# Batch 0's phi and K over two queues in head halves, and the constants of ones on GpSimd, at the start of a fused attention and channel-mix kernel

## The chip, the cores and the metric

The kernel runs on one core of a Trainium2 chip. Five engines work beside each other, each on its own list of instructions: TensorE (PE in the profile, its weight loads PEld), VectorE (DVE), ScalarE (ACT), GpSimd (POOL) and SyncE (SP), which only issues DMAs here. The metric is device time in microseconds, the median of several runs; lower is better.

## What is computed

For each of 8 batches and 8 heads, 576 tokens of width 64 attend through 32 memory slots; the result goes through a gated channel mix (d_model 512, d_ff 1024).

```python
# attention: q, k, v (8, 8, 576, 64), phi (8, 8, 576, 32)
a = exp(phi - max);  a = a / (sum(a, axis=2) + 1e-09)
k_m = einsum('bhsm,bhsd->bhmd', a, k);  v_m = einsum('bhsm,bhsd->bhmd', a, v)
attn = softmax(scale * q @ k_m.T)
x = (attn @ v_m)            # heads side by side: (8, 576, 512)
# channel mix
xk = mu_k * x + (1 - mu_k) * x_prev;   xr = mu_r * x + (1 - mu_r) * x_prev
k = relu(xk @ w_k);   v = k * k @ w_v;   r = sigmoid(xr @ w_r)
out = r * v
```

## The kernel before

The order of all work is written out by hand. `PLAN` (L19 to L85) is one long list of words; the loop at L800 runs through it and issues what each word stands for. `0:mu` is a step of batch 0, `c0:6a` a block of the key matmul, `b:1x8@3` a number of filler matmuls (`keep_busy`, L255, into PSUM bank 3), `p:q:0b` a preload. A word that comes twice is a step in two parts: the matmuls, and later what unloads them. Each engine works through its instructions in the order of issue; a wait for data stops everything behind it on that engine. PE's list at the start, by PLAN, is: 10 fillers of 512 columns (`WARM`, L262), three more, the transpose of mu (`0:mu`, L276), two fillers, the sums of exp(phi) (`0:z`, L321), six fillers, the K products of head groups 0 and 1 (`0:kg0`, L311), three fillers, those of head groups 2 and 3 (`0:kg1`), one filler, the broadcast of mu (`0:mub`, L267), and so on. The fillers multiply a tile of zeros and their results are not used.

Batch 0 is loaded first, ahead of PLAN. Phi goes as one DMA of 576 KB on ScalarE's queue (`load_phi`, L182), then K as two DMAs of 576 KB each, head groups 0 and 1, then 2 and 3 (`k0`, L184 and L185). Both arrive as float32. SyncE's queue carries mu_k and mu_r, 2 KB each, into `mu2` (L188, L189). ScalarE then takes exp of phi, second half of the head groups first (`0:exp1`, `0:exp0`, L291). K is turned to bf16 by `cast_k` (L296): groups 0, 1 and 2 on ScalarE (`0:c00`, `0:c01`, `0:c10`), group 3 on VectorE (`0:c11`), where the cast stands ahead of the copy of mu (L278) and the reciprocal of the sums (L325). `kg0` needs c00 and c01, `kg1` needs c10 and c11.

GpSimd issues all other loads, which change float32 to bf16 on the way. Its list begins with `PRE` (L91, run at L230):

```python
PRE = "after: id: q:0a"
```

`after` copies one element of `mu2` into `mark` (L211), a tile that nothing reads, so that GpSimd goes on when mu is in; `id` makes the identity matrix (a memset and a select); `q:0a` is the first part of q of batch 0. PLAN's preloads follow (q's second part, V in two halves, the weights, phi of batch 1 and so on).

VectorE clears `zeros` (L186), which the fillers read, then casts from the identity (`ident_f`, `sel`) and writes two constants: `ones` (L236 and L238, three memsets), the right-hand side of `0:z`, and `sumh` (L243 and L246, five memsets), which the denominators (L419) use.

Of the kernel before, what the change touches and what calls it, by code (L numbers as in the profile page):

```python
# [10 lines left out]
F32 = mybir.dt.float32  # L11
BF16 = mybir.dt.bfloat16
# [75 lines left out]

WARM = (10, 8)

PRE = "after: id: q:0a"  # L91
TAIL = ("o:72",)
WHOLE = {"o:71a": "scalar", "o:71b": "sync"}
ONE = ("o:32", "o:30", "o:33", "o:31", "o:42",)
# [3 lines left out]
NJ = 9  # L98
# [5 lines left out]
def kernel(  # L104
# [13 lines left out]
    nc = tc.nc  # L118
    B, H, S, D = q.shape
    M = phi.shape[-1]  # L120
# [15 lines left out]
    const = ctx.enter_context(tc.sbuf_pool(name="const", bufs=1))  # L136
    big = ctx.enter_context(tc.sbuf_pool(name="big", bufs=1))
    ld = ctx.enter_context(tc.sbuf_pool(name="ld", bufs=2))
# [19 lines left out]
    HH = H // 2  # L158
    ROWS = (slice(0, 64), slice(64, 128))
# [2 lines left out]
    q0s = [const.tile([128, HH, w, D], BF16, name=f"q0{w}") for w in (5, 4)]  # L162
    ems = [const.tile([128, NJ, HH, M], BF16, name=f"em{i}") for i in range(2)]
    identity = const.tile([128, 128], BF16, name="identity")
    mark = const.tile([1, 1], F32, name="mark")
    zeros = const.tile([128, 128], BF16, name="zeros")


    loads = {}

    def rows(src):
        return src.rearrange("h s d -> (h s) d").rearrange("(a p j) d -> p a (j d)", a=HH, j=NJ)

    def load_phi(b, eng):
        ph = ld.tile([128, HH, NJ, M], F32, name="ph", tag="ph")
        eng.dma_start(out=ph.rearrange("p h j m -> p h (j m)"), in_=rows(phi[b]))
        loads[b] = ph

    def load_rows(dst, src):
        nc.gpsimd.dma_start(out=dst.rearrange("p h j d -> p h (j d)"), in_=rows(src))  # L180

    load_phi(0, nc.scalar)  # L182
    k0 = work.tile([128, HH, NJ, D], F32, name="k0f", tag="G", bufs=2)
    for gs in (slice(0, 2), slice(2, 4)):  # L184
        nc.scalar.dma_start(out=k0[:, gs].rearrange("p h j d -> p h (j d)"), in_=rows(k[0])[:, gs])  # L185
    nc.vector.memset(zeros, 0.0)  # L186
    mu2 = const.tile([2 * ND, 128], F32, name="mu2")
    nc.sync.dma_start(out=mu2[:ND, :], in_=moe_mu_k.rearrange("(a b) -> a b", b=128))  # L188
# [12 lines left out]
    def preload(word):  # L201

        what, _, part = word.partition(":")
        if what in weights:
            dst, src = weights[what]
            f0, f1 = (int(x) * 128 for x in part.split("-"))
            nc.gpsimd.dma_start(out=dst[:, :, f0:f1], in_=src[:, :, f0:f1])
        elif what == "id":
            make_identity(nc, identity)
        elif what == "after":  # L210
            nc.gpsimd.tensor_copy(mark, mu2[:1, :1])  # L211
        else:
            n = int(part[0])
            if what == "phi":
                load_phi(n, nc.gpsimd)
            else:
                dst = qs[n % 2].rearrange("p (h j) d -> p h j d", j=NJ) if what == "q" else kvs[n % 2][:, "kv".index(what)]
                src = {"q": q, "k": k, "v": v}[what][n]
                if part[1:] in ("a", "b"):
                    x = "ab".index(part[1])  # L220
                    js = HALVES[x]
                    nc.gpsimd.dma_start(out=q0s[x].rearrange("p h j d -> p h (j d)"),
                                        in_=rows(src)[:, :, js.start // QR * D:js.stop // QR * D])
                elif part[1:] in ("g", "h"):
                    gs = slice(0, 2) if part[1] == "g" else slice(2, 4)
                    nc.gpsimd.dma_start(out=dst[:, gs].rearrange("p h j d -> p h (j d)"), in_=rows(src)[:, gs])
                else:
                    load_rows(dst, src)

    for word in PRE.split():  # L230
        preload(word)

    ident_f = const.tile([2 * ND, 2 * ND], F32, name="identf")
    nc.vector.tensor_copy(ident_f, identity[:2 * ND, :2 * ND])
    ones = const.tile([128, 2], BF16, name="ones")
    nc.vector.memset(ones, 0.0)  # L236
    for hg in range(2):
        nc.vector.memset(ones[ROWS[hg], hg:hg + 1], 1.0)  # L238

    sel = const.tile([2 * ND, 2 * HH, M], F32, name="sel")  # L240
    nc.vector.tensor_copy(sel, identity[:2 * ND, :2 * HH].unsqueeze(2).to_broadcast([2 * ND, 2 * HH, M]))
    sumh = const.tile([128, 4, M], BF16, name="sumh")
    nc.vector.memset(sumh, 0.0)  # L243
    for g in range(4):
        r = slice(g * M, (g + 1) * M)
        nc.vector.memset(sumh[r, g, :], 1.0)  # L246
    mu1 = const.tile([128, 2 * ND], F32, name="mu1")
    mu_m = const.tile([128, 2, 2, 2, D], F32, name="mu_m")

# [550 lines left out]
    for word in " ".join(PLAN).split():  # L800
        word, _, used = word.partition("@")
        word, _, now["by"] = word.partition("/")
        now["banks"] = iter(used)
        who, _, name = word.partition(":")
        if who == "p":
            preload(name)
        elif who == "w":
            queues[:] = [nc.sync]
            store(name, outs[name], slice(0, Dm))
        elif who == "b":  # L810
            keep_busy(*map(int, name.split("x")))
        else:
            now["whole"] = word in WHOLE or word in ONE
            if word in WHOLE:
                queues[:] = [getattr(nc, WHOLE[word])]
            elif len(queues) != 1 + (word in TAIL) or queues[0] is not nc.sync:
                queues[:] = [nc.sync, nc.scalar][:1 + (word in TAIL)]
            parts = pending.pop(word, None) or (mixes[who][name] if who in mixes else attend[int(who)](name))()
            if hasattr(parts, "send") and next(parts, who) is not who:
                pending[word] = parts  # L820
# [31 lines left out]
```

## Time and profile before

| what | value |
|---|---|
| time, median of 3 runs | 189.22 us (189.16 to 189.24) |
| span of the profiled execution | 187.4 us |
| median less span | 1.8 us |
| packets of the software queue (GpSimd's loads) | 20.45 MB, 59.1% of 16 engines' span |
| packets of ScalarE's queue (q10) | 2.08 MB, 3.4% |
| packets of SyncE's queue (q1) | 9.00 MB, 17.3% |

The span runs from the first to the last instruction of one execution taken by the hardware profiler. The time of that execution by itself is not among the numbers; the median is that of unprofiled runs of the same kernel. A row of the timeline or of the chain gives the start and the duration in us, then engine, line and operation; x9 means nine instructions merged into one row, whose duration reaches from the first start to the last end. In square brackets stands how long the engine was idle before, and what ended the wait. ACTq, SPq and POOL with DMA_DIRECT2D are issues of DMAs, not the transfers. A filler's row is "idle L258": that is the name of its PSUM tile; PE works then.

### The profile page before, as it was taken

The page shows a single profiled execution, that of the slowest core. Times are in us where ns is not written, and L with a number is a line of the kernel's source. Part 1 is how long each engine was busy: PE and PEld are TensorE (multiplying, and loading weights), DVE is VectorE, ACT ScalarE, POOL GpSimd, SP SyncE. Part 2 cuts the span into 40 slices and gives each one's busy share as a digit, 9 for nine tenths or more (in the row PEclk, how much of TensorE's full clock was granted, in tenths as well). Part 3 has the DMA queues.
Part 4 walks back from the last instruction along what each step waited for, and adds up shares of the span by engine and source line. Part 5 has one row for each costly group of instructions (what it writes and reads, how often), then busy time and mean ns, then how long its engine had stood idle before and what let it go on. Part 6 is the DMA issues. An engine that isn't in the chain of part 4 may idle for free.

```text
span 187.4 us, 5998 instructions
## 1 busy us (share of the span) xinstructions
PE 180.2 (96%) x2459; PEld 102.9 (55%) x2481; DVE 158.9 (85%) x344; ACT 146.5 (78%) x352; POOL 30.0 (16%) x46
## 2 busy tenths in 40 slices
PE   7998998999999999999999999999999999999992
PEld 2454764667645565556554755655535563474451
DVE  2265877999999999999999999987999999989441
ACT  2638866879999999999998999868998887656500
POOL 5843522121310450110103000000000000000000
PEclk9999999999999999999999999999999999999998
DMA  5999999999999999999999992142203421240254
GB/s 181 288 204 270 203 207 203 252 222 208 287 218 272 231 230 344 258 268 270 272 180 155 200 263 66 33 112 59 58 0 80 93 59 43 70 112 3 56 139 141
DMA packets 24940, 31.91 MB, mean 170 GB/s; under 512 B 1897, under 2 KB 19057, under 8 KB 24913
## 3 DMA queue, kind: packets, MB, share of 16 engines
q0 software_dynamic: 17936, 20.45, 59.1%
q1 hardware_dynamic: 5680, 9.00, 17.3%
q10 hardware_dynamic: 1296, 2.08, 3.4%
q8 instruction: 19, 0.31, 0.6%
q14 instruction: 9, 0.07, 0.1%
HBM read 38.28 MB, written 9.44 MB: 255 GB/s over the span
## 4 chain that ended last, share of the span: by engine, by line
PE 96%; issue 1%; ACT 1%; DVE 1%; ACTq 0%
PE pv L759 33%; PE pk L616 8%; PE pk L624 7%; PE pb L624 7%; PE idle L258 7%; PE gps L491 6%; PE kvps L311 4%; PE pk L598 4%; PE pb L686 3%; PE pr L686 3%; PE pr L678 3%; PE pr L708 2%; PE scps L394 2%; PE pr L665 2%; PE zps L321 1%
## 5 line engine op out<-in xcount | busy, mean ns | idle before, releaser
L759 PE MATMUL pv<-wv,sq 128*128 128x512 bf16 (+3 forms) x285 | 59.3, 350 | 0.5
L759 PEld LDWEIGHTS <-sq 128*128 128x128 bf16 x296 | 27.6, 98 | 25.6 <-issue 2.4
L497 ACT CAST G<-gps 128x512 bf16<-128x512 f32 x60 | 32.0, 632 | 2.4 <-PE gps L491 2.3
L770 DVE SCALAR_TENSOR_TENSOR o<-sg,pv 128x512 f32<-128x512 f32 (+3 forms) x41 | 24.9, 612 | 6.8 <-PE pv L759 6.7
L624 PEld LDWEIGHTS <-G 128*128 128x128 bf16 x224 | 21.4, 98 | 8.7 <-issue 0.6
L624 PE MATMUL pk<-diff,G 128*128 128x288 bf16 x112 | 22.9, 286 | 0.1
L624 PE MATMUL pb<-diff,G 128*128 128x288 bf16 x112 | 22.9, 286 | 0.0
L620 ACT COPY pb<-pk 128x288 f32<-128x288 f32 x49 | 19.4, 423 | 4.0 <-PE pk L616 1.9
L582 ACT ACTIVATE rl<-pb 128x288 bf16<-128x288 f32 x43 | 18.2, 432 | 4.5 <-PE pb L624 4.2
L590 DVE TENSOR_TENSOR sq<-rl 128x576 bf16<-128x576 bf16 (+2 forms) x49 | 19.3, 417 | 1.7 <-ACT rl L582 1.4
L616 PE MATMUL pk<-atn,G 128*128 128x288 bf16 x112 | 19.9, 286 | 0.2
L582 ACT ACTIVATE rl<-pk 128x288 bf16<-128x288 f32 (+2 forms) x44 | 18.5, 429 | 1.7 <-PE pk L598 0.6
L497 DVE CAST G<-gps 128x512 bf16<-128x512 f32 x24 | 15.6, 680 | 0.4 <-PE gps L491 0.3
L588 ACT ACTIVATE sq<-rl 128x576 bf16<-128x576 bf16 (+2 forms) x23 | 14.5, 640 | 0.1
L457 DVE TENSOR_TENSOR atn<-e,lz 128x576 bf16<-128x576 bf16 (+2 forms) x18 | 12.1, 682 | 2.9 <-ACT lz L429 2.8
L258 PE MATMUL idle<-zeros 128*128 128x512 bf16 (+2 forms) x45 | 13.5, 421 | 1.1 <-DVE zeros L186 1.0
L500 DVE TENSOR_TENSOR G<-G 128x1024 bf16<-128x1024 bf16 x21 | 14.1, 678 | 0.2
L655 ACT ACTIVATE sg<-pr 128x512 f32<-128x512 f32 x22 | 13.5, 621 | 0.9 <-PE pr L686 0.5
L616 PEld LDWEIGHTS <-G 128*128 128x128 bf16 x112 | 10.6, 98 | 6.3 <-issue 0.8
L584 DVE TENSOR_SCALAR rl<-pk 128x288 bf16<-128x288 f32 (+2 forms) x28 | 12.4, 452 | 1.5 <-PE pk L598 0.7
L380 DVE STREAM_TRANSPOSE qT<-q 128x576 uint32<-128x576 uint32 (+2 forms) x16 | 12.1, 764 | 0.0
L291 ACT ACTIVATE em<-ph 128x1152 bf16<-128x1152 f32 (+1 forms) x9 | 9.8, 1104 | 1.6 <-DMA ph<-in_phi_dram 1.6
(101 smaller groups left out, 275.6 us busy)
## 6 DMA issues: line engine op xcount, KB each, us to landing
out_dram<-o SPq DMA_DIRECT2D x48, 128.0 KB, 2.4
ph<-in_phi_dram POOLq DMA_DIRECT2D x7, 576.0 KB, 15.3
kv<-in_k_dram POOLq DMA_DIRECT2D x7, 576.0 KB, 15.6
q<-in_q_dram POOLq DMA_DIRECT2D x7, 576.0 KB, 15.9
kv<-in_v_dram POOLq DMA_DIRECT2D x7, 576.0 KB, 18.2
out_dram<-o SPq DMA_DIRECT2D x20, 64.0 KB, 5.1
out_dram<-o SPq DMA_DIRECT2D x5, 256.0 KB, 5.4
k0f<-in_k_dram ACTq DMA_DIRECT2D x2, 576.0 KB, 6.5
```

What stands on the lines that cost most here:

```text
L258: nc.tensor.matmul(ps.rearrange("p (a b) -> p a b", b=64), lhsT=zeros, rhs=zeros[:, :64].unsqueeze(1).to_broadcast([128, blocks, 64]), sta ...
L497: return lambda: copier()(g_tile()[:, v, c, GCOLS[i]], st["gps", v, i][c])
L500: return lambda: nc.vector.tensor_sub(g_tile()[:, 1, :, GCOLS[i]], g_tile()[:, 2, :, GCOLS[i]], g_tile()[:, 0, :, GCOLS[i]])
L582: nc.scalar.activation(rl, ps, AF.Relu, scale=HALF ** 0.5)
L588: nc.scalar.activation(dst, rl, AF.Square)
L590: nc.vector.tensor_mul(dst, rl, rl)
L616: nc.tensor.matmul(pa, lhsT=st["G"][:, 2, c, f], rhs=st["at"][:, c, :NP], start=c == 0, stop=False, skip_group_check=True)
L620: copier()(pb, pa)
L624: nc.tensor.matmul(ps, lhsT=st["G"][:, v, c, f], rhs=st["d"][:, kind, c], start=False, stop=c == 1, skip_group_check=True)
L655: nc.scalar.activation(gated[name], ps, AF.Tanh, scale=0.5)
L759: nc.tensor.matmul(pv[:, cols], lhsT=squares, rhs=wv_sb[:, fi, cols], start=(fi == 0), stop=(fi == NF - 1))
L770: nc.vector.scalar_tensor_tensor(o[:, cols], in0=gated[name][:, cols], scalar=1.0, in1=pv[:, cols], op0=AL.add, op1=AL.mult)
```

## The change

Batch 0's phi and K are each loaded in two halves by head groups: groups 0 and 1 on SyncE's queue, 2 and 3 on ScalarE's, phi first on both. The two loads of mu stay on SyncE's queue and so stand behind its two halves. The copy into `mark` is gone, so GpSimd no longer waits for mu; in its place GpSimd writes `ones` and `sumh` with eight memsets, after the identity and before its first load. VectorE's memsets of these two are gone. PLAN stays as it is.

```diff
-PRE = "after: id: q:0a"
+PRE = "id: ones: q:0a"
...
-    mark = const.tile([1, 1], F32, name="mark")
...
+    ones = const.tile([128, 2], BF16, name="ones")
+    sumh = const.tile([128, 4, M], BF16, name="sumh")
+
+    def ones_tiles():
+        nc.gpsimd.memset(ones, 0.0)
+        for hg in range(2):
+            nc.gpsimd.memset(ones[ROWS[hg], hg:hg + 1], 1.0)
+        nc.gpsimd.memset(sumh, 0.0)
+        for g in range(4):
+            r = slice(g * M, (g + 1) * M)
+            nc.gpsimd.memset(sumh[r, g, :], 1.0)
...
-    load_phi(0, nc.scalar)
+    ph0 = ld.tile([128, HH, NJ, M], F32, name="ph", tag="ph")
+    loads[0] = ph0
     k0 = work.tile([128, HH, NJ, D], F32, name="k0f", tag="G", bufs=2)
-    for gs in (slice(0, 2), slice(2, 4)):
-        nc.scalar.dma_start(out=k0[:, gs].rearrange("p h j d -> p h (j d)"), in_=rows(k[0])[:, gs])
+    for dst, src in ((ph0, phi), (k0, k)):
+        for eng, gs in ((nc.sync, slice(0, 2)), (nc.scalar, slice(2, 4))):
+            eng.dma_start(out=dst[:, gs].rearrange("p h j d -> p h (j d)"), in_=rows(src[0])[:, gs])
     nc.vector.memset(zeros, 0.0)
...
-        elif what == "after":
-            nc.gpsimd.tensor_copy(mark, mu2[:1, :1])
+        elif what == "ones":
+            ones_tiles()
...
-    ones = const.tile([128, 2], BF16, name="ones")
-    nc.vector.memset(ones, 0.0)
-    for hg in range(2):
-        nc.vector.memset(ones[ROWS[hg], hg:hg + 1], 1.0)
...
-    sumh = const.tile([128, 4, M], BF16, name="sumh")
-    nc.vector.memset(sumh, 0.0)
-    for g in range(4):
-        r = slice(g * M, (g + 1) * M)
-        nc.vector.memset(sumh[r, g, :], 1.0)
```

## The prediction

> **What bounds the kernel now.** I read the page's busy table and its chain that ended last first, then the chain in order of time over the first 17 us, because everything that the change touches is issued there.
>
> ```profile
> PE 180.2 (96%) x2459; PEld 102.9 (55%) x2481; DVE 158.9 (85%) x344; ACT 146.5 (78%) x352; POOL 30.0 (16%) x46
> PE 96%; issue 1%; ACT 1%; DVE 1%; ACTq 0%
> ```
>
> TensorE is the bound from end to end: 96% of the chain is PE itself. A start that is later by some time is therefore later at the end by nearly the same, unless PE later waits for something that does not move with it. The start as the chain shows it (start, duration, what):
>
> ```profile
> 0.99 5.06 PE idle L258 x13
> 6.06 0.15 PE psmu L276
> 6.21 0.38 PE idle L258 x2
> 6.59 0.25 PE zps L321 x9
> 6.84 1.12 PE idle L258 x6
> 7.96 0.04 issue
> 8.00 0.45 PE kvps L311 x36
> 8.45 0.75 PE idle L258 x3
> 9.21 0.47 PE kvps L311 x36
> 9.67 0.16 PE idle L258
> 9.83 0.64 PE mub L267 x4
> ...
> 14.70 0.38 issue
> ```
>
> The reader is to see that PE hardly waits here. It runs a fixed list: filler matmuls (L258) of a number written into PLAN, then the transpose of mu (psmu), fillers, the sums of exp(phi) (zps), fillers, and the two halves of the K products (kvps, kg0 and kg1). Data that come earlier do not shorten this list, since the change takes no filler out; data that come later stretch it. The gaps that an earlier load could close are the 0.04 us at 7.96 and, at most, the 0.38 us at 14.70.
>
> How close the data are is in the timeline of ScalarE, VectorE, SyncE's queue and GpSimd (start, duration, engine and line, in brackets the idle time before and who ended it):
>
> ```profile
> 0.24 0.10 POOL L836 MEMSET const-float32-0.0<- 128x1 f32 x1 [0.24 <-issue]
> 0.35 0.10 POOL L836 MEMSET const-uint8-127<- 128x1 uint8 x1
> 0.74 0.45 ACTq L176 DMA_DIRECT2D ph<-in_phi_dram  x1
> 0.75 0.37 SPq L188 DMA_DIRECT2D mu<-in_moe_mu_k_dram  x1
> 0.83 0.11 DVE L186 MEMSET zeros<- 128x64 uint32 x1 [0.83 <-PEq L836]
> 1.18 0.26 SPq L189 DMA_DIRECT2D mu<-in_moe_mu_r_dram  x1
> 1.22 1.04 ACTq L185 DMA_DIRECT2D k0f<-in_k_dram  x2
> 2.15 0.17 POOL L211 COPY mark<-mu 1x1 f32<-1x1 f32 x1 [1.71 <-DMA mu<-in_moe_mu_k_dram]
> 2.27 0.19 POOL masks.py:197 MEMSET identity<- 128x128 bf16 x1
> 2.54 0.29 POOL masks.py:199 TENSOR_SCALAR_AFFINE_SELECT identity<-identity 128x128 bf16<-128x128 bf16 x1
> 2.85 1.65 POOL L222 DMA_DIRECT2D q<-in_q_dram  x2
> 3.98 0.47 DVE L246 MEMSET sumh<- 32x32 bf16 x4
> 5.15 1.25 ACT L291 ACTIVATE em<-ph 128x576 bf16<-128x576 f32 x2 [1.58 <-DMA ph<-in_phi_dram]
> 6.59 1.25 ACT L296 CAST kv<-k0f 128x576 bf16<-128x576 f32 x2 [0.18 <-DMA k0f<-in_k_dram]
> 8.33 0.67 ACT L296 CAST kv<-k0f 128x576 bf16<-128x576 f32 x1 [0.50 <-DMA k0f<-in_k_dram]
> 8.33 0.85 DVE L296 CAST kv<-k0f 128x576 bf16<-128x576 f32 x1 [3.88 <-DMA k0f<-in_k_dram]
> ```
>
> So phi (576 KB) is in at 5.15, K's first half (576 KB) at 6.59 and its second half at 8.33. The first half is just in time: its two casts end at 6.59 + 1.25 = 7.84, and kg0 starts at 8.00 behind fillers that end at 7.96, a slack of 0.12 us. mu is in before 2.15, far ahead of psmu at 6.06.
>
> **The change part by part.**
>
> Phi and K. Now the order is phi, first half, second half on one queue, and the first half is served before the second. Afterwards SyncE's queue holds phi's first half and K's first half, ScalarE's the other halves. The bytes are the same 1,728 KB, so what matters is whether two queues are faster than one, and who is served first. The stages of one microsecond (us, busy times, granted clock, DMA share, GB/s), and the queues between 6 and 7 and between 7 and 8 us:
>
> ```profile
> 2.00:3.00 1.00, 1.00 (x4) 0.30 (x2) 0.14 (x2) 0.71 (x1) 0.74 (x4) 1.00 0.84 204
> 4.00:5.00 1.00, 1.00 (x4) 0.41 (x3) 0.33 (x4) 0.00 (x0) 1.00 (x2) 1.00 1.04 400
> 6.00:7.00 1.00, 1.00 (x15) 0.65 (x15) 0.00 (x0) 0.82 (x2) 1.00 (x2) 1.00 1.07 390
> q0 software_dynamic: 26, 0.02, 11.9%
> ...
> q0 software_dynamic: 225, 0.14, 103.8%
> q10 hardware_dynamic: 43, 0.08, 21.9%
> ```
>
> From 4 us on ScalarE's queue alone (q10) fills the engines at 400 GB/s; 576 KB at that rate are 1.47 us, and 6.59 - 5.15 = 1.44 us. There is no spare rate for a second queue in K; only between 2 and 3 us, at 204 GB/s and a share of 0.84, could two queues gain some tenths. The second half took 8.33 - 6.59 = 1.74 us, with GpSimd's queue (q0) beside it. The trace has no two hardware queues with big loads at once, so I bound K's first half from both sides: 6.59 if it is still served first, 8.33 if it ends with the second. Two equal queues that start together end together; I take 6.59 + 1.44 = 8.03. Its casts (c00, c01) then end at 9.28 and kg0 starts near 9.3: **+1.3 us**. The third cast, c10, runs on ScalarE behind them, 0.67 more, to 9.95, while kg1 is due at 9.3 + 0.45 + 0.75 = 10.5: hidden. c11 on VectorE starts near 8.05 instead of 8.33 and is needed by none earlier. Phi's two halves are together in by about 5.1 as before.
>
> The Trainium skill speaks against a gain here: "DMA: Bandwidth & Descriptors", section Rules for kernel authors, says that spreading DMAs over the issuing engines does not help bandwidth and saves only issue time. The 400 GB/s of one queue agree; by it the whole load ends where it ended, as in my sum.
>
> mu. Its two loads stay on SyncE's queue, but now behind two issues of about 0.45 and 0.52 us (0.74 and 1.04/2 above): issued at 1.7 instead of 0.75. That alone would be harmless, 1.7 + (2.15 - 0.75) = 3.1. But the queue ahead of it now holds 864 KB, and the other queue as much. The trace of before has no small load behind a big one on SyncE's queue. Bounds: 3.1 if it overtakes, 8.33 if it waits for all. The nearest row for waiting behind other queues is q0: issued from 2.85 on, it moved 26 packets up to 7 us and 225 in the next, when ScalarE's queue ran dry. I take mu as waiting for most of the load, 7.8: on the engines that carry it, it comes after their share of SyncE's halves, and engines finish between 7 and 8. PE stands at psmu in order; behind it are 2 fillers, zps, 6 fillers, kg0: 8.00 - 6.06 = 1.94 us. From 7.8 that puts kg0 at 9.74, **+1.7 us**, later than K's 9.3. The two delays lie beside each other, so the larger counts: +1.7, with +1.3 as the lower and 8.33 + 1.94 - 8.00 = +2.3 as the upper end. If SyncE's halves were served in the order phi, phi, K first half, mu, K second half, both would be about 6.6 and the price 6.6 + 1.94 - 8.00 = +0.6.
>
> While PE waits at psmu, zps and its fillers queue behind it; exp(phi) goes on on ScalarE, and VectorE's copy of psmu (9.10 before) stands behind c11 anyway.
>
> GpSimd. Gone: the copy to mark and the wait of 1.71 us. It can start the identity when VectorE starts, 0.83: memset to select 0.27, select to the DMA issue 0.31, by the starts above. Added: eight memsets between them and q's first load. Bounds for one: 0.036 (four constants between 0.24 and 0.35) and 0.27 (the identity's memset); I take 0.10, nearest to the small ones' duration: 0.8 us. q's load is issued at 0.83 + 0.58 + 0.8 = 2.2 instead of 2.85, 0.65 us earlier (from 1.15 earlier to 0.7 later). Worth nothing: q0's packets start as the hardware queues drain, and PE waits for no load of GpSimd's in the start. If they did start sooner, they would share the engines with K and push it later, up to 8.33.
>
> VectorE. Its memsets of ones and sumh leave: cost nothing, gain nothing, since VectorE sits idle for 3.88 us before c11. ones is needed by zps at 6.59 and is there at about 2.2.
>
> Afterwards. Everything behind kg0 is PE's own chain and engines fed by it, so the delay stays. Only the 0.38 us at 14.70 could be absorbed if what PE waits for there does not move; I leave it in. Sum: +1.7 us on a span of 187.4, whose execution has no time of its own in what I read; the median of the three runs is 189.22, 1.8 above the span, which I take as fixed. 189.22 + 1.7 = 190.9.
>
> **The rivals.**
>
> *Served in turn.* K's first half and mu at 6.6, as worked out above: 189.8. For it: issues alternate in time, first halves first. Against it: both queues have all issued by 1.8, so the engines have both to choose from. The skill's rule in "DMA: Bandwidth & Descriptors", section Queues, rings and completion order, is that an engine goes round its queues packet by packet, which speaks for ending together; no run shown so far settles it.
>
> *The clock drops.* PE idles 1.7 us shortly after it became fast (13 fillers in 5.06 us, then 6 in 1.12). If the clock falls to half for a stretch of some 3.4 us, at most 1.7 us come on top: 192.6. The granted clock near the end (same columns):
>
> ```profile
> 183.30:186.70 3.40, 0.60 (x4) 0.18 (x2) 0.52 (x1) 0.00 (x0) 0.00 (x0) 0.97 0.59 174
> 186.80:187.40 0.60, 0.00 (x0) 0.00 (x0) 0.00 (x0) 0.00 (x0) 0.00 (x0) 0.50 0.00 0
> ```
>
> It fell to 0.50 only behind 3.4 us with 0.60 us of work; half a stretch of work is more than that, which speaks against. "TensorE: Matmul & The Clock Gate", Part 1 of the Trainium skill, gives windows of about 3.4 us; the trace agrees, at 3.4.
>
> *No change.* mu overtakes (in by 6.06 + 0.38 = 6.4) and K's first half is in by 6.59 + 0.12 + 0.38 = 7.1: then PE is late by under 0.4, and the time 189.2 to 189.6. For it: mu is 2 KB a load. Against: 864 KB ahead of it.
>
> *Faster.* One mechanism: two queues fill the slow stage between 2 and 3 us, so all is in early, and GpSimd's loads, 0.65 us earlier, close the gap at 14.70. Price 0.38 + 0.04: 188.8. It decides only if mu is in by 6.06 and K's first half by 6.71; for the whole load that means 1,728 KB in some 4 us from 2.1, 440 GB/s, more than the 400 of the fullest stage.
>
> **How the numbers follow.** Forecast (190.5 to 191.5) 0.53, served in turn 0.17, clock 0.08, no change 0.13, faster 0.09. Slower by over 0.2% (0.38 us, about what a measurement of this kernel can tell from no change) sums to 0.78. The range reaches from 189.4, within the case of no change, to 192.4, most of the clock's case.
>
> **What would show it.** Right: psmu starts behind a PE wait that a mu load ends, well after 6.06; ScalarE's first K cast starts near 8 instead of 6.59; kg0 near 9.7; later stages the same durations shifted. Wrong: psmu still at 6.06 (mu overtook); the first cast still at 6.6 (served in turn); fillers of double length after the wait (clock); or a shift that is gone by 20 us (absorbed).

## The result and the profile after

The changed kernel took 192.57 us (median of 4 runs, 191.27 to 192.87), the kernel before 189.23 beside it: ratio 1.016, 95% interval 1.0124 to 1.0196. A repeat with more runs (the last but two of the experiments below) gave 1.0116, interval 1.0088 to 1.0144. One execution of the repeat (194.36 us) and one of a later experiment (194.64 us) lie over 1.5% above the fastest of their kernel and count as slow, so the ratios leave them out. The change makes the kernel slower by 1 to 2%. The profiled execution has a span of 190.6 us instead of 187.4.

The chain of the changed kernel in order of time (start, duration, what), where before the fillers ran through to psmu at 6.06:

```profile
2.22 5.04 DMA mu<-in_moe_mu_r_dram
7.26 0.14 issue
7.39 0.19 PE psmu L279
7.59 0.38 PE idle L261 x2
7.97 0.20 PE zps L324 x9
8.17 1.87 PE idle L261 x6
10.04 0.04 issue
10.09 0.67 PE kvps L314 x29
10.75 1.28 PE idle L261 x3
12.03 0.38 PE kvps L314 x36
12.41 0.16 PE idle L261
12.57 0.64 PE mub L270 x4
```

The reader is to see two things. The chain begins with a DMA now: mu's second load, issued at 2.22, takes 5.04 us, and PE waits for it. And behind psmu the same six fillers that took 1.12 us take 1.87, the three after kg0 1.28 instead of 0.75. From mub on the rows have their old durations, but for the gap that the prediction named (0.38 us at 14.70): it is 0.45 us at 17.43 now, so nothing is absorbed there. The start of mub tells how much is lost by then: 12.57 - 9.83 = 2.74 us, of which 7.39 - 6.06 = 1.33 is the later psmu and the other 1.41 the longer rows.

ScalarE's and VectorE's timeline of the changed kernel, and below it PE's wait from the list of waits (us in total, times, longest):

```profile
4.96 1.26 ACT L294 ACTIVATE em<-ph 128x576 bf16<-128x576 f32 x2 [1.86 <-DMA ph<-in_phi_dram]
7.75 1.82 ACT L299 CAST kv<-k0f 128x576 bf16<-128x576 f32 x3 [1.53 <-DMA k0f<-in_k_dram]
8.07 0.85 DVE L299 CAST kv<-k0f 128x576 bf16<-128x576 f32 x1 [6.37 <-DMA k0f<-in_k_dram]
```

```profile
PE psmu L279 <- DMA mu<-in_moe_mu_r_dram: 1.6, 1, 1.6
```

Phi is in at 4.96 (5.15 before), K's halves at 7.75 and 8.07 (6.59 and 8.33 before): the whole load ends a little sooner, and its first needed half ends 1.16 us later.

The windows of the changed kernel (us, then PE, PEld, DVE, ACT, POOL busy, granted clock, DMA share, GB/s):

```profile
5.00:6.00 1.00, 0.76 (x5) 0.15 (x2) 0.00 (x0) 1.00 (x2) 1.00 (x2) 1.00 1.03 401
6.00:7.00 1.00, 0.00 (x0) 0.00 (x0) 0.00 (x0) 0.21 (x1) 1.00 (x2) 1.00 1.08 353
8.00:9.00 1.00, 1.00 (x11) 0.41 (x9) 0.93 (x3) 1.00 (x3) 0.64 (x1) 0.69 1.38 195
9.00:10.00 1.00, 1.00 (x4) 0.27 (x2) 0.06 (x1) 0.56 (x1) 0.27 (x1) 0.50 1.43 201
10.00:11.00 1.00, 0.94 (x38) 0.64 (x38) 0.00 (x0) 0.00 (x0) 0.48 (x1) 0.50 1.25 208
12.00:13.00 1.00, 1.00 (x42) 0.89 (x41) 0.52 (x2) 0.00 (x0) 0.50 (x1) 1.00 1.23 209
```

PE is empty between 5.76 and 7.39; a little later, from about 8.4 to 11.8, its granted clock is 0.50, though PE works all the time by then. That is the second loss.

A third is at the other end. VectorE's last instruction ends at 186.72 + 0.52 = 187.24, and the span 3.4 us later; before it was 183.93 + 0.52 = 184.45 and 3.0 us. The waits of SyncE's queue at the end, first before, then after:

```profile
SPq L847 <- DMA out_dram<-o: 1.6, 1, 1.6
```

```profile
SPq L850 <- DMA out_dram<-o: 2.0, 1, 2.0
```

So 1.33 + 1.41 + 0.4 make 3.1 of the 3.2 us between the spans.

### The profile page after: what moved, and what is told of

It is laid out like the page before. It is cut to its first block, busy times and chain, and to the rows that moved or that the text cites. A ratio compares the mean times of both kernels' runs of the same rounds, so it can differ in the third digit from the quotient of the medians.

```text
span 190.6 us, 6021 instructions
## 1 busy us (share of the span) xinstructions
PE 182.4 (96%) x2481; PEld 103.2 (54%) x2481; DVE 158.1 (83%) x336; ACT 146.3 (77%) x352; POOL 30.9 (16%) x53
## 4 chain that ended last, share of the span: by engine, by line
PE 93%; DMA 3%; issue 1%; SPq 1%; ACT 0%; DVE 0%; ACTq 0%
PE pv L762 33%; PE pk L619 7%; PE pk L627 7%; PE pb L627 7%; PE gps L494 6%; PE idle L261 4%; PE kvps L314 4%; PE pk L601 4%; PE pr L689 3%; PE pr L681 3%; PE pb L689 3%; DMA mu<-in_moe_mu_r_dram 3%; PE pr L711 2%; PE pr L668 2%; PE scps L397 2%; PE zps L324 1%
## 5 line engine op out<-in xcount | busy, mean ns | idle before, releaser
L762 PE MATMUL pv<-wv,sq 128*128 128x512 bf16 (+3 forms) x296 | 60.4, 351 | 0.0
L261 PE MATMUL idle<-zeros 128*128 128x512 bf16 (+2 forms) x45 | 14.5, 446 | 1.1 <-DVE zeros L198 1.0
```

Source lines behind the costliest of these rows:

```text
L261: nc.tensor.matmul(ps.rearrange("p (a b) -> p a b", b=64), lhsT=zeros, rhs=zeros[:, :64].unsqueeze(1).to_broadcast([128, blocks, 64]), sta ...
L762: nc.tensor.matmul(pv[:, cols], lhsT=squares, rhs=wv_sb[:, fi, cols], start=(fi == 0), stop=(fi == NF - 1))
```

## The experiments

Theory after the result: (1) mu, behind 864 KB on SyncE's queue, holds PE; (2) if it did not, K's later first half would hold PE nearly as long; (3) PE's stand, its idle wait at psmu, makes the clock drop for one stretch of 3.4 us; (4) GpSimd's part is free. Rivals: mu alone counts; the long fillers come from DMA traffic; GpSimd's earlier loads cost time.

**mu first on SyncE's queue.** The three lines of `mu2` stand ahead of the loads of phi and K:

```diff
+    nc.sync.dma_start(out=mu2[:ND, :], ...)   # mu_k, then mu_r, both first
     for dst, src in ((ph0, phi), (k0, k)):
         for eng, gs in ((nc.sync, slice(0, 2)), (nc.scalar, slice(2, 4))):
```

> The changed kernel with the two mu loads issued first on SyncE's queue, ahead of the halves of phi and K. If mu's wait on PE (1.64 us before psmu) is the main cause, psmu is back near 6.1 and PE stands instead at kg0 until K's first half, in at about 7.8, is cast: kg0 near 9.2, +1.2 us over the kernel before, 190.4; with a clock drop behind that stand, about 191.6. If mu alone were the cause and K's order harmless, 189.2.

191.66 us, ratio 1.0113 (1.0077 to 1.0149): no return to 189. Its ScalarE and VectorE, and from the chain its kg0:

```profile
5.49 0.46 DVE L299 CAST kv<-k0f 128x576 bf16<-128x576 f32 x1 [3.78 <-DMA k0f<-in_k_dram]
6.07 0.68 ACT L294 ACTIVATE em<-ph 128x576 bf16<-128x576 f32 x1 [1.67 <-DMA ph<-in_phi_dram]
8.42 1.25 ACT L299 CAST kv<-k0f 128x576 bf16<-128x576 f32 x2 [1.67 <-DMA k0f<-in_k_dram]
```

```profile
9.71 0.44 PE kvps L314 x34
```

PE stands at kg0 now, which starts at 9.71, later than expected (here, and below where the casts hold kg0, without its first two matmuls, which run before the second cast is done). SyncE's halves are issued 0.7 us behind ScalarE's, and that decides the order: ScalarE's K half is in at 5.49, before SyncE's half of phi (6.07), and SyncE's K half only at 8.42. The queues' packets show it directly: between 3 and 4 us ScalarE's queue moved 191 packets and SyncE's 4; in the changed kernel, where both start together, 179 and 137. Its profile has a drop of the clock too (granted 0.50 between 12 and 13 us), but the three other executions, at 0.996 to 0.999, took 191.08 to 192.19 us, so the drop is not what keeps this kernel above 189. So mu is not the only cause.

**GpSimd's part alone.** Phi, K and mu loaded as before; `PRE = "id: ones: q:0a"` and `ones_tiles` as changed.

> Phi and K on ScalarE's queue in the old order, mu first on SyncE's; GpSimd writes ones and sumh and does not wait for mu. My theory: this part costs and brings nothing, 189.2 (189.0 to 189.4), psmu at 6.06 and kg0 at 8.0 as before. Rival: GpSimd's earlier loads take DMA share from K, K's halves land later and kg0 with them: 189.6 or more.

189.57 us beside 189.54 for the kernel before, ratio 1.0007 (0.9992 to 1.0022), kg0 at 8.10, K's halves in at 6.50 and 8.16: this part is worth nothing either way, as argued.

**mu late, K in order.** The kernel above, with mu's two loads on ScalarE's queue behind K (`nc.sync` becomes `nc.scalar` in both).

> As the kernel with GpSimd's part alone, but the two mu loads stand behind K on ScalarE's queue: phi and K arrive in the old order, only mu is late. If a small load behind big ones on its queue waits for them, mu lands near 8.2 and psmu runs near 8.3: +2.2 us, and with a clock drop for one stretch of 3.4 us some 1.3 more: 191.4 without, 192.7 with it. If mu can overtake: psmu near 6.1 and 189.2.

193.27 us (median of four), ratio 1.0223 (1.0169 to 1.0277). The profiled execution had full clock and 191.42 us:

```profile
2.94 5.18 DMA mu<-in_moe_mu_r_dram
8.12 0.14 issue
8.26 0.19 PE psmu L277
8.45 0.38 PE idle L259 x2
8.83 0.20 PE zps L322 x9
9.04 1.12 PE idle L259 x6
10.15 0.04 issue
10.20 0.45 PE kvps L312 x36
```

A load of 2 KB lands only when nearly all that its queue holds ahead of it is in: at 8.12 here, while ScalarE's cast of K's second half starts at 8.36 (in the changed kernel 7.26 and 7.75). kg0 is late by 10.20 - 8.00 = 2.2 us with K nearly on time (6.73 and 8.36). Here PE stood longer than in the changed kernel (1.8 us against 1.6 in the lists of waits), and yet the fillers behind took 1.12 us. The other three had 192.84 and 193.69 us at a granted clock of 0.991 and 194.64 at 0.980.

**The stand filled with work.** The changed kernel with one number changed:

```diff
-WARM = (10, 8)
+WARM = (17, 8)
```

> The changed kernel with 17 instead of 10 warm-up fillers, so that PE works in most of the stand before psmu. Theory: the clock then stays at full speed, psmu stays near 7.4, the six fillers behind it take 1.1 instead of 1.9 us, kg0 near 9.4, and the time falls by about 1.4 us to 191.2 or less although PE does more. Rival (the six fillers and kg0 are slow by DMA traffic or by late K casts, not by the clock): the time stays at 192.6 or rises.

190.68 us, ratio 1.0064 (1.0043 to 1.0085); all six executions had a granted clock of 1.0. The chain:

```profile
1.00 6.75 PE idle L261 x20
7.76 0.15 PE psmu L279
7.91 0.38 PE idle L261 x2
8.29 0.20 PE zps L324 x9
8.49 1.12 PE idle L261 x6
9.61 0.04 issue
9.65 0.45 PE kvps L314 x36
```

PE executes seven more matmuls, psmu is even later, and the kernel is faster than the changed one by 0.5 to 1.0% going by the ratios (1.0064 against 1.0116 in the repeat and 1.016), which is 1.0 to 1.8 us. Between the two profiles 1.17 us of this is there by mub (11.40 and 12.57). Another half us comes later, where the gap of 0.45 us at 17.43 is missing here; the trace names no cause for that gap. DMA traffic is what it was (1.40 of share between 8 and 9 us, 1.38 in the changed kernel), so it is not what made the fillers long: the stand was, by way of the clock.

**psmu later in PLAN.** Loads as changed; the word moves behind kg0:

```diff
-... b:1x8@5 0:mu@4 b:1x8@2 b:1x2@1 0:exp0 0:z@0 ... 0:kg0@16 b:2x8@2 ...
+... b:1x8@5 b:1x8@2 b:1x2@1 0:exp0 0:z@0 ... 0:kg0@16 0:mu@4 b:2x8@2 ...
```

> The changed kernel, loads as changed, but psmu moved in PLAN from ahead of the sums of exp(phi) to behind kg0. mu's lateness then stops nobody; what is left is K's first half, cast by about 9.0. Theory: PE stands for about 1.4 us at kg0 instead of 1.6 at psmu, kg0 near 9.05 (+1.05): 190.4 at full clock, up to 191.7 with a clock drop, so the two delays lie beside each other and taking one away saves little. Rival (mu alone is the cause): 189.2 to 189.5.

190.83 us, ratio 1.0074 (1.005 to 1.0099), at full clock in the profile:

```profile
7.95 1.25 ACT kv L299 x2
9.20 0.04 issue
9.24 0.44 PE kvps L314 x34
```

kg0 starts at 9.24, held by K's casts, which start at 7.95. The two delays do lie beside each other: with mu out of the way K's half still costs 1.2 us.

**mu shared out first.** mu_k first on SyncE's queue, mu_r first on ScalarE's.

> The changed kernel with mu_k first on SyncE's queue and mu_r first on ScalarE's, so that mu is early and neither queue leads. Theory: psmu near 6.1; both K halves end together near 7.9, kg0 at 9.2, 190.4 to 191.7 by the clock. If instead a lead of some tenths decides the order, as in the kernel with mu first on SyncE's queue alone, ScalarE's half comes first (VectorE's cast starts near 5.5) and K's first half after 8.3.

190.26 us, ratio 1.0032 (1.0017 to 1.0046), better than I expected: SyncE's half of phi goes out at 1.18, ScalarE's at 1.33, and this lead of 0.15 us brings K's first half in at 7.30, a full microsecond ahead of the second (8.30). Where both queues start within 0.02 us of each other, the halves are 0.2 to 0.6 us apart in four profiles. kg0 starts at 8.60. That the lead does it is read from this one profile.

**K by single groups, fewer fillers.** As the last, K as four loads (groups 0 and 1 first), and `b:2x8@1` taken out between the sums and kg0.

> As the kernel with mu shared out first, but K goes one head group at a time, groups 0 and 1 ahead of 2 and 3 on the two queues, and PLAN has two fillers of 512 columns less between the sums and kg0. Theory: K's first half is in at about 6.3 and the second by 7.9, kg0 starts near 7.6 and kg1 near 8.75 instead of 9.21: 0.4 us less than before. Rival: the queues do not keep this order, a group of the first half comes after 7.5, kg0 at 8.8 or later, 190 or more.

189.91 us, ratio 1.0028 (1.0013 to 1.0044): the gain did not come, and the rival's numbers did not either (kg0 at 7.99, not 8.8). Group 0 was in by 6.15, but group 1, on the other queue, at 7.26, and groups 2 and 3 at 8.64 and 8.82, later than the 8.33 of the kernel before. kg1 started at 9.36.

**Before, with fewer fillers.** `b:2x8@1` taken out of the kernel before.

> The kernel before with the same two fillers left out. Theory: kg0 is then held by K's first casts (7.84) and kg1 by the cast of the second half (9.18): kg1 near 9.2 as before and the time unchanged within 0.1 us. Rival: PE is held by its fillers alone and not by K, then kg1 is 0.4 us earlier and the time with it.

189.41 us, ratio 0.9998 (0.9985 to 1.0012): no change, as the theory has it. Its profile doesn't settle why: the early fillers ran longer there (psmu at 6.40), so the fillers ended at 7.87, by the casts' end.

**The changed kernel again.**

> The changed kernel once more, for the share and the size of the clock's part. Theory: its executions fall in two groups by the granted clock, those with about 1.0 near 191.2 (the wait alone, some 1.6 over the kernel before) and those near 0.99 at 192.4 to 192.9 (a stretch of 3.4 us at half clock on top, some 1.4). Rival: the clock changes nothing and the times spread without regard to it.

192.05 us (median of six), ratio 1.0116 (1.0088 to 1.0144). The ten executions of the changed kernel, from both sets:

| granted clock, mean of the span | times, us |
|---|---|
| 1.0 | 191.04, 191.22, 191.27 |
| 0.995 | 191.45 |
| 0.988 to 0.991 | 192.37, 192.64, 192.78, 192.87, 193.10 |
| 0.980 | 194.36 |

The medians of the first and the third row differ by 192.78 - 191.22 = 1.56 us. At full clock the change costs about 191.2 - 189.3 = 1.9 us; in six of the ten the drop comes on top. The last row is near what two stretches of 3.4 us at half clock would give (an estimate: 1 - 3.4 / 192.6 = 0.982). The 72 executions of the kernel before that ran beside the experiments have no granted clock below 0.996.

**mu first on ScalarE's queue.** The mirror of the first.

> The changed kernel with both mu loads first on ScalarE's queue, the mirror of the kernel with mu first on SyncE's queue. If the queue that starts some tenths earlier is served first, now SyncE's halves come first: K's first half is in by about 6, but phi's second half only near 6, so that exp(phi), whose second half goes first on ScalarE, is late: the sums near 7.4, the first K casts from 7.4 to 8.6, kg0 near 8.7, 190.2. If the queues share evenly: phi by 5.1, K's halves together at 7.8, kg0 at 9.1 and 190.5 or more.

191.94 us, ratio 1.0134 (1.01 to 1.0168); 191.03 and 191.23 at full clock. ScalarE and VectorE:

```profile
6.14 1.26 ACT L294 ACTIVATE em<-ph 128x576 bf16<-128x576 f32 x2 [2.25 <-DMA ph<-in_phi_dram]
7.30 1.80 ACT L299 CAST kv<-k0f 128x576 bf16<-128x576 f32 x3
8.14 0.79 DVE L299 CAST kv<-k0f 128x576 bf16<-128x576 f32 x1 [6.43 <-DMA k0f<-in_k_dram]
```

Both expectations were too low. PE waits 1.15 us for the late exp(phi), and kg0 starts at 8.99 instead of 8.7; 0.4 us of the rest is the longer end that the next run explains, and 0.45 the gap at 14.70 of before, which is 0.83 us long here. The picture turns round: now ScalarE's half of phi is the late one (6.14), while K's first half waits for ScalarE (the first cast has no idle time before it) and the second is in at 8.14. The queue that starts first is served first.

**One more load in the kernel before.** mu_r as two DMAs of two rows:

```diff
-    nc.sync.dma_start(out=mu2[ND:2 * ND, :], in_=moe_mu_r.rearrange("(a b) -> a b", b=128))
+    for i in (0, 2):
+        nc.sync.dma_start(out=mu2[ND + i:ND + i + 2, :], in_=moe_mu_r.rearrange("(a b) -> a b", b=128)[i:i + 2])
```

> The kernel before with mu_r loaded as two DMAs of two rows instead of one of four: one DMA more on SyncE's queue, as in the changed kernel, and nothing else. Theory: DMAs of SyncE's and ScalarE's queues take eight semaphores in turn; one more load moves the last store from the eighth to the first of them, and SyncE at the end waits for them in order, some 0.06 us each. So the start is as before (psmu 6.0 to 6.4, kg0 near 8.0), but the time from the end of VectorE's last instruction to the end of the span grows from 3.0 to 3.35 us, and the time by 0.4 us, about 0.2%. Rival (the longer tail of the changed kernel has to do with SyncE's big loads or the late start): tail 3.0 and the time unchanged.

190.03 us, ratio 1.0029 (1.0008 to 1.0051). kg0 is at 8.07, as before. VectorE's last instruction, from the timeline, and SyncE's wait at the end, from the list of waits:

```profile
184.24 0.52 DVE L771 SCALAR_TENSOR_TENSOR o<-sg,pv 128x352 f32<-128x352 f32 x1 [0.82 <-PE pv L760]
```

```profile
SPq L848 <- DMA out_dram<-o: 2.1, 1, 2.1
```

The span is 188.2, so the tail, from VectorE's end to the span's, is 188.2 - 184.76 = 3.4 us: one small DMA at the start costs some 0.4 us at the end. The changed kernel has one DMA more on these queues too. All profiles agree: with five loads on the two queues the tail is 2.9 to 3.0 us (four kernels, one of them with kg0 2.2 us late), with six or eight 3.3 to 3.4 us (eight kernels).

## Why the prediction was right, and where it was not

The direction and the place were right: slower, at the start, by loads that come later in the queues than before, on a PE list whose fillers hide nothing when data are late. The time was not: the median of 192.57 lies above the forecast of 190.5 to 191.5 and 0.2 us above the range's upper end of 192.4, the repeat's 192.05 inside the range. Executions at full clock took 191.04 to 191.27, inside the forecast, but partly by luck: a term too large by 0.4 us (mu) stands against one left out of 0.4 us (the end).

**K.** Expected at 8.03 for the first half, in at 7.75; all of K in at 8.07 by two queues instead of 8.33 by one. That two queues carry the same bytes in nearly the same time is borne out. Its price by itself, +1.3 by the sum, was 1.2 us at kg0 with psmu out of the way.

**mu.** The step held in kind: it came behind most of the load ahead of it, and the larger delay counted. Its size was too large: in at about 7.3 rather than 7.8, half a microsecond before SyncE's K half, psmu late by 1.33, where the sum had 1.7. mu alone would put kg0 at 7.39 + 1.94 = 9.33, K alone put it at 9.24, so the two delays were nearly equal.

**The clock.** Here the prediction failed. It gave the drop a chance of 0.08, because at the end of the kernel before the clock fell only behind a stretch with 0.60 us of work in 3.4. Its step "half a stretch of work is more than that, which speaks against" did not hold. A stand of 1.64 us in the profile went with a drop, and six of ten executions had one, the others not; the stretch has a fixed length (3.4 us at 0.50) but no fixed place against the kernel's start (from 8.3 us in the changed kernel, 8.0 in its repeat, 11.7 with mu first on SyncE's queue, two microseconds after the last stand there). The 3.4 us just ahead of these three drops hold 1.77, 1.49 and 2.18 us of matmul work, far more than the 0.60 at the end of the kernel before. "TensorE: Matmul & The Clock Gate" of the Trainium skill, Part 1, has this window as free-running; the two groups of times agree with that. Its price was named rightly, at most 1.7: 1.41 in the profile, 1.56 between the groups. With the measured sizes the sum is 189.23 + 1.33 + 1.41 + 0.4 = 192.37, the time of the profiled execution.

**The end.** "1.8 above the span, which I take as fixed" and "the delay stays" left out the 0.4 us of the tail, which has nothing to do with the start. The run with one more small load shows that the count of DMAs sets it; that it goes by the order in which SyncE waits for eight semaphores at the end fits SyncE's longer wait, but is argued: no row shows that order, and it was not tried.

**GpSimd and VectorE.** Nothing gained, nothing lost: 1.0007. The memsets were sized too small: in the changed kernel the eight run from 1.26 to 2.65 us, 1.4 us instead of 0.8, and q's load goes out at 2.59 instead of 2.2.

**The rivals.** "Served in turn" did not come in the changed kernel (7.75 and 8.07), but with a lead of 0.15 us it came in part (7.30 and 8.30, where in turn would be 6.6). Its price was slightly misadded: 6.6 + 1.94 - 8.00 is 0.54, not 0.6; the 189.8 stands. The rule of the Trainium skill that the prediction named ("DMA: Bandwidth & Descriptors", Queues, rings and completion order), a round between queues, would have the two end together; with a lead the runs show otherwise, and the measurement decides. "No change" and "faster" needed mu by 6.4; no run with mu behind big loads had it.

What stays open: which threshold of idle time drops the clock (with mu late and K in order, PE stood 1.85 us and the clock stayed at 1.0; whether a stand falls into one stretch or is split between two could decide, but that is argued only), why the queue that leads keeps its lead, and what PE waits for in the gap at 14.70 of before, which is absent with the stand filled and 1.07 us long in the repeat's profile. No version tried beats the kernel before.

## What to carry to other kernels

A small load that an in-order engine needs early goes ahead of the big ones on its queue; here 2 KB issued at 2.2 us, behind 864 KB, landed at 7.3. Splitting one served order over two queues brought all data slightly sooner here and the first needed data later, so ask for the first one, not the last. And a stand of the matrix engine can cost twice, once as the wait and once by the clock behind it: useless matmuls in the wait made this kernel 1.0 to 1.8 us faster.

## What the runs showed of the hardware

The queue that starts first wins by far more than its lead: 0.7 us of head start made 288 KB of phi on the other queue land at 6.07 instead of 4.96, behind the leader's 576 KB of K, with 191 packets to 4 between 3 and 4 us, while leads under 0.02 us left the two K halves 0.2 to 0.6 us apart. And a DMA of 1 KB at the start of a kernel made its end 0.4 us longer.
